# A chunked retention and gated feed-forward kernel: the same operations issued in another order, the gate-value rows in six smaller buffers, seven output buffers

## The chip, the cores and the metric

The kernel runs on one core of a Trainium2 chip. The metric is the device time of one execution in microseconds (us). Before the change three executions took 233.48, 233.62 and 234.39 us, median 233.62 us. Engines are called as in the profile: PE (matrix multiply), PEld (its weight load), DVE, ACT and POOL (elementwise engines), SP (issues transfers only); POOL also issues transfers. Each engine works through its own queue strictly in the order in which it was given its instructions.

## The reference

A retention layer over four sequences of 768 tokens with eight heads of 64, then a normed, gated feed-forward layer without bias over all 3072 tokens:

```python
for t in range(S):                                   # S = 768
    state = gamma * state + einsum('bhd,bhe->bhde', k[:, :, t], v[:, :, t])
    y[:, :, t] = scale * einsum('bhd,bhde->bhe', q[:, :, t], state)
x = y.transpose(0, 2, 1, 3).reshape(B * S, H * D)    # 3072 x 512
xn = x / sqrt(mean(x * x, -1) + 1e-6) * rms_g
g, val = xn @ w_gate, xn @ w_val                     # 512 x 1536 each
out = (g * sigmoid(g) * val) @ w_out                 # 1536 x 512
```

Inputs and output are float32. `gamma` is a constant per head.

## The kernel before

The 768 tokens are cut into six chunks `c` of 128. Per chunk and sequence `b` (0 to 3) the recurrence becomes matrix products. Scores of the chunk (`A`, two PSUM banks per sequence) are masked by DVE (`M0`, `M1`), multiplied with v (`Y`, with the carried state added from chunk 1 on), squared and summed on ACT (`S`), turned into a row factor on POOL (`R`), normed on DVE (`N`) and transposed, by PE and a copy (`X`, `XE`) in chunks 0 and 1, by a transposing transfer of SP (`XE` with `@S`) after that. `K`, `U` and `B` carry the state. Then the feed-forward part of the chunk: gate and value products of 128 hidden columns (`g`, `v`), Silu on ACT (`s`), their product on DVE into the rows `hT` (`h`), the second product (`d`, at the very end `e`), the copy out of PSUM (`o`) and the store (`st`). q and k are loaded (`Lq`, `Lk`), transposed by PE (`Tq`, `Tk`) and copied (`Eq`, `Ek`) in chunks 0 and 1, converted (`Cq`, `Ck`) and transposed by SP's transfers (`tq`, `tk`) later. `D` scales k for the state, `J` transposes one key block back.

Nothing schedules at run time or at build time: a string `ORDER` holds all operations by hand, and a loop at the end of the kernel issues them one after another. `g.0.6.7.0.4/4` is the gate product of chunk 0, hidden blocks 6 to 7, sequences 0 to 4, in PSUM bank 4; `Ck.0.2@D` is a conversion on DVE. The position of an operation in the string is its position in its engine's queue. Waits between engines follow from the data and from the buffers: a ring of n buffers makes the n+1st user wait for the last reader of one of them, and a PSUM bank is free when what lies in it has been read. The operations `H.n` and `hot.n` multiply constants; nobody reads their result, they only keep PE busy where it would be idle.

POOL's queue issues the loads of chunk 0 and 1 and of all weights (`wg`, `wv`, `wo`), which convert to bfloat16 on the way, and does `R`, `B` and some conversions between them. SP's queue issues chunk 2 to 5's loads, the transposing transfers and the stores; the loads of chunk 2 wait until the last part of `wo` has landed (`after`). ACT loads the table of Silu with the operation `tab`.

```python
for w in ORDER.split():
    w, _, bk = w.partition("/")
    w, _, en = w.partition("@")
    f, *a = w.split(".")
    F[f](ENG.get(en), [int(i) for i in bk], *map(int, a))
```

Of the kernel before, what the change touches and what calls it, by code (L numbers as in the profile page):

```python
# [9 lines left out]
F32 = mybir.dt.float32  # L10
BF16 = mybir.dt.bfloat16
AF = mybir.ActivationFunctionType
ALU = mybir.AluOpType
# [4 lines left out]
H.8/3 yt Lk.0.2@S ident Ck.0.2@D vd Lk.1.1@S iota Tk.0.2/0 rms.1@S D.0.2@D Lk.0.0@P Lq.0.1@P H.3/1 Tk.0.0/2  # L18
H.1/1 Tq.0.1/7 Ek.0.0@D mk1 hot.3/1 J.0.0/3 D.0.0@D mk0 Lq.0.0@P Lk.0.1@P Tq.0.0/6 Lq.0.2@P Eq.0.1@A Eq.0.0@A
Tk.0.1/5 Ek.0.1@A Ek.0.2@D yd Lk.0.3@P H.1/1 Tq.0.2/4 tab Lq.0.3@P Eq.0.2@D hot.2/0 A.0.0/5017 M0.0.0 G/2 M1.0.0  # L20
Tq.0.3/6 Lv.0.0@P M0.0.1 GE@A Tk.0.3/3 Eq.0.3@A Lv.0.1@P M1.0.1 Lv.0.2@P Lv.0.3@P wg.0.2 Y.0.0/4 wv.0.2 A.0.2/21
wg.2.4 M1.0.2 Ek.0.3@A Lq.1.1@P H.3/0 A.0.3/61 S.0.0 M0.0.2 H.1/0 Y.0.2/3 K.0.0/0 J.0.1/5 M1.0.3 R.0.0 S.0.2
N.0.0 M0.0.3 Y.0.1/1 H.1/2 X.0.0/4 J.0.3/7 wv.2.4 S.0.1 XE.0.0@D U.0.0@A R.0.2 R.0.1 Ck.1.1@A N.0.2 B.0.0 H.2/2
Y.0.3/0 g.0.0.2.0.1/2 K.0.2/6 S.0.3 s.0.0.2.0.1 N.0.1 U.0.2@A wg.4.6 X.0.2/4 R.0.3 XE.0.2@D D.0.1@D
v.0.0.2.0.1/3 X.0.1/2 wv.4.6 causal XE.0.1@A Lk.1.2@P v.0.0.2.2.3/4 wg.6.9 Lq.1.2@P wv.6.9 h.0.0.2.0.1
g.0.0.2.2.3/6 D.0.3@D Lq.1.0@P g.0.0.2.1.2/5 g.0.2.3.0.3/3 s.0.0.2.2.3 h.0.0.2.2.3 s.0.0.2.1.2 g.0.3.4.0.3/6
N.0.3 v.0.0.2.1.2/4 D.1.1@D Tq.1.1/5 Lk.1.0@P Tk.1.1/0 X.0.3/7 Eq.1.1@D K.0.1/2 wg.9.12 v.0.3.4.0.3/1 Lv.1.1@P
s.0.3.4.0.3 XE.0.3@A g.0.0.4.3.4/6 s.0.2.3.0.3 h.0.0.2.1.2 g.0.4.6.3.4/4 wv.9.12 g.0.4.5.0.3/7 v.0.4.6.3.4/5
v.0.2.3.0.3/3 U.0.1@D s.0.4.6.3.4 Ek.1.1@A h.0.3.4.0.3 g.0.5.6.0.3/0 s.0.4.5.0.3 h.0.4.6.3.4 mc.0@P mc.1@P
# [48 lines left out]
v.3.11.12.0.4/7 h.3.11.12.0.4 K.4.1/4 Lv.5.1@S Y.4.2.2 S.4.1 Y.4.3.2 S.4.2 V.5.1@P d.3.1.0.10/6 tk.5.3 tk.5.2
N.4.0 R.4.1 tk.5.1 st.2.0@S d.3.1.10.12 S.4.3 tq.5.3 N.4.1 R.4.3 o.3.1@A R.4.2 d.3.0.0.10/1 B.4.3 N.4.3 Lq.5.1@S
# [24 lines left out]
def kernel(  # L104
# [530 lines left out]
```

## Time and profile before

| | before |
|---|---|
| time, median of 3 | 233.62 us (233.48 to 234.39) |
| profiled execution, first to last instruction | 233.6 us |
| PE busy | 227.6 us (97%) |
| DVE / ACT / POOL busy | 130.4 / 96.1 / 89.7 us |
| first gate product starts | 19.38 us |
| transfers, mean | 144 GB/s, 33.61 MB |

The profiled execution's span is the median of the timed ones to within 0.1 us, so span and time are used alike. The page shows the busy shares of the engines over time, the clock that PE was granted, and the chain of work that ended last. A busy PE is not a PE at its best: the windows of the profile, which give busy time and clock by stage, and the idle times shown behind an instruction in the order of time say more.

### The profile page before, as it was taken

Reading aid. Unit: us, or ns where it says so; the run is one execution under the profiler, and the core shown is the slowest. Engines: PE = TensorE matmul, PEld = TensorE weight load, DVE = VectorE, ACT = ScalarE, POOL = GpSimd, SP = SyncE. Lnnn points to the kernel's source line nnn. Section 1 sums busy time; section 2 is a strip of 40 time slices with the busy share of each in tenths; the row PEclk is TensorE's granted clock in tenths of the full one; section 3 lists DMA queues with packets and bytes.
Section 4 is the critical chain, followed back from the end, with each engine's and each line's share of the span. In section 5 each row is a group of like instructions: output and inputs, shape, how many; then the busy total and the mean of one; then the engine's idle time right before and its main releaser. Section 6 shows DMA issues by size and latency. Waiting matters only on the chain.

```text
span 233.6 us, 4637 instructions
## 1 busy us (share of the span) xinstructions
PE 227.6 (97%) x1771; PEld 120.8 (52%) x1771; DVE 130.4 (56%) x241; ACT 96.1 (41%) x231; POOL 89.7 (38%) x163
## 2 busy tenths in 40 slices
PE   8799999999999999999999999999999999999994
PEld 2458855645545655445554444554455444444444
DVE  6479639753662965628975239866367532323320
ACT  7658433514337231464731346553265332232202
POOL 8958998550544555030273741247003100000000
PEclk9979999999999999999999999999999999999999
DMA  7999999999798888999988899968511400020222
GB/s 126 147 180 123 127 179 184 205 145 215 133 206 214 171 194 140 262 218 221 235 173 146 179 221 206 198 149 142 148 61 27 112 0 0 3 90 9 83 89 93
DMA packets 105353, 33.61 MB, mean 144 GB/s; under 512 B 94449, under 2 KB 102385, under 8 KB 105330
## 3 DMA queue, kind: packets, MB, share of 16 engines
q1 hardware_dynamic: 81858, 25.70, 50.2%
q0 software_dynamic: 23472, 7.60, 30.1%
q8 instruction: 14, 0.23, 0.4%
q14 instruction: 9, 0.07, 0.1%
HBM read 28.31 MB, written 6.29 MB: 148 GB/s over the span
## 4 chain that ended last, share of the span: by engine, by line
PE 89%; DMA 4%; POOL 2%; ACT 2%; DVE 1%; issue 0%; SPq 0%; POOLq 0%; DVEq 0%; ACTq 0%
PE v_ps L549 27%; PE g_ps L549 27%; PE o_ps L574 21%; PE a_ps L403 3%; DMA kb<-in_k_dram 3%; PE y_ps L441 2%; PE kv_ps L526 2%; PE y_ps L445 2%; DMA out_dram<-o_sb 1%; PE o_ps L596 1%; PE hot_ps L240 1%; PE t_ps L366 1%; PE t_ps L371 1%; PE xt_ps L495 1%; ACT xsq L455 1%; ACT xsq L458 1%
## 5 line engine op out<-in xcount | busy, mean ns | idle before, releaser
L567 DVE TENSOR_TENSOR hT<-sg,v_ps 128x512 bf16<-128x512 bf16 (+2 forms) x76 | 48.7, 656 | 47.8 <-PE v_ps L549 34.8
L549 PE MATMUL v_ps<-xnT,wv_b 128*128 128x512 bf16 (+2 forms) x344 | 71.2, 345 | 0.1
L559 ACT ACTIVATE sg<-g_ps 128x512 bf16<-128x512 f32 (+2 forms) x76 | 42.1, 575 | 70.6 <-PE g_ps L549 68.1
L549 PE MATMUL g_ps<-xnT,wg_b 128*128 128x512 bf16 (+2 forms) x344 | 70.0, 344 | 0.0
L574 PE MATMUL o_ps<-wo_b,hT 128*128 128x512 bf16 x276 | 63.5, 379 | 0.0
L549 PEld LDWEIGHTS <-wg_b 128*128 128x128 bf16 x344 | 30.4, 98 | 29.3
L549 PEld LDWEIGHTS <-wv_b 128*128 128x128 bf16 x344 | 30.2, 98 | 28.9 <-DVE am L426 0.6
L574 PEld LDWEIGHTS <-hT 128*128 128x128 bf16 x276 | 26.3, 98 | 29.1
L468 POOL TENSOR_SCALAR ms<-ssq 128x1 f32<-128x1 f32 x24 | 4.6, 190 | 59.1 <-ACT xsq L458 58.4
L426 DVE TENSOR_TENSOR am<-a_ps,causal 128x512 bf16<-128x512 f32 x32 | 20.6, 685 | 7.8 <-PE a_ps L403 7.5
L339 POOL TENSOR_TENSOR qb<-qf,ydec 128x512 bf16<-128x512 f32 x13 | 14.0, 1074 | 25.2 <-DMA qf<-in_q_dram 24.9
L146 ACT COPY o_sb<-o_ps 128x512 f32<-128x512 f32 (+1 forms) x16 | 8.8, 552 | 29.7 <-PE o_ps L574 23.1
L458 ACT ACTIVATE xsq<-y_ps 128x512 f32<-128x512 f32 x22 | 13.2, 599 | 18.9 <-PE y_ps L445 13.7
L482 DVE SCALAR_TENSOR_TENSOR xn<-y_ps,rstd,g_bc 128x512 bf16<-128x512 f32 x22 | 16.3, 748 | 4.3 <-POOL rstd L470 3.0
L146 DVE COPY o_sb<-o_ps 128x512 f32<-128x512 f32 (+1 forms) x10 | 6.4, 648 | 18.1 <-PE o_ps L574 12.2
L541 POOL CAST st_b<-st_f 64x256 bf16<-64x256 f32 x40 | 15.9, 398 | 1.3
L470 POOL TENSOR_TENSOR rstd<-ms,mhalf 128x1 f32<-128x1 f32 x24 | 13.3, 552 | 2.0
L534 DVE TENSOR_TENSOR st_f<-st_f,kv_ps 128x512 f32<-128x512 f32 x16 | 10.8, 684 | 5.2 <-PE kv_ps L526 4.6
L356 ACT ACTIVATE vp<-vf,vdec 128x64 bf16<-128x64 f32 x48 | 12.2, 343 | 0.0
L426 DVE TENSOR_TENSOR am<-a_ps,mask 128x512 bf16<-128x512 f32 x16 | 10.4, 686 | 2.5 <-PE a_ps L403 2.3
L240 PE MATMUL hot_ps<-one 128*128 128x512 bf16 x20 | 8.5, 547 | 1.1 <-DVE one L153 1.1
L441 PEld LDWEIGHTS <-am 128*128 128x128 bf16 x176 | 7.8, 99 | 3.1 <-issue 0.3
(99 smaller groups left out, 174.8 us busy)
## 6 DMA issues: line engine op xcount, KB each, us to landing
out_dram<-o_sb SPq DMA_DIRECT2D x23, 256.0 KB, 2.4
kf<-in_k_dram SPq DMA_DIRECT2D x18, 256.0 KB, 3.8
qf<-in_q_dram SPq DMA_DIRECT2D x16, 256.0 KB, 3.9
vf<-in_v_dram SPq DMA_DIRECT2D x16, 256.0 KB, 3.9
wo_b<-in_moe_w_out_dram POOLq DMA_DIRECT2D x3, 512.0 KB, 12.2
qb<-in_q_dram POOLq DMA_DIRECT2D x8, 128.0 KB, 6.6
vp<-in_v_dram POOLq DMA_DIRECT2D x8, 128.0 KB, 6.5
kb<-in_k_dram POOLq DMA_DIRECT2D x6, 128.0 KB, 5.9
```

The costliest lines, as they stand in the source:

```text
L146: (e.copy if e is ACT else e.tensor_copy)(out, in_)
L339: e.tensor_tensor(out=u["qb"], in0=u["qf"], in1=ydec[:, c, :, None].to_broadcast([128, H, D]), op=ALU.mult)
L426: DVE.tensor_tensor(out=u["am"][:, i], in0=u["a"][i], in1=m, op=ALU.mult)
L441: nc.tensor.matmul(y[:, h, :], u["am"][:, h % 2, h // 2, :], u["vp"][:, h, :], start=h == 0, stop=c == 0 and h == H - 1, skip_group_check= ...
L458: ACT.activation(xsq, flat(u["y"]), AF.Square, accum_out=u["ssq"])
L470: POOL.tensor_tensor(out=u["rstd"], in0=ms, in1=mhalf, op=ALU.pow)
L482: DVE.scalar_tensor_tensor(out=u["xn"], in0=flat(u["y"]), scalar=u["rstd"], in1=g_bc, op0=ALU.mult, op1=ALU.mult)
L541: POOL.tensor_copy(st_b[b][r, :, i * 64:i * 64 + 64], st_f[b][r, :, i * 64:i * 64 + 64])
L549: nc.tensor.matmul(p[:, (n - n0) * m:(n - n0 + 1) * m], W[w][0][:, s, n * 128:(n + 1) * 128], xnT[c][:, s, b0 * C:b1 * C], start=s == 0, s ...
L559: ACT.activation(sg[:, :cols], done["wg", c, n0, b0][:, :cols], AF.Silu)
L567: DVE.tensor_tensor(out=hT[c][:, n0:n1, b0 * C:b1 * C], in0=sg, in1=p, op=ALU.mult)
L574: nc.tensor.matmul(o_ps[c, b], hT[c][:, n, b * C:(b + 1) * C], wo_b[:, n, :], start=n == 0, stop=n == NFF - 1)
```

## The change

The string `ORDER` is replaced by another one with the same operations, on partly other engines and in other PSUM banks. Three places of the code go with it. The second half of `ident`, a DVE copy that makes `pick` (PE's operand for `Tq` and `Tk` in chunk 0), becomes an operation of its own. The rows `hT` of a chunk, before one tile of 12 blocks in a ring of two, become three tiles of 4 blocks each in a ring of six: the same memory, set free by thirds. The output ring grows from four to seven buffers, and many stores stand much later in SP's queue.

```diff
 ORDER = """
-H.8/3 yt Lk.0.2@S ident Ck.0.2@D vd Lk.1.1@S iota Tk.0.2/0 rms.1@S D.0.2@D Lk.0.0@P Lq.0.1@P H.3/1 Tk.0.0/2
...
+H.1/0 Lk.0.1@P H.1/1 Lk.0.2@S Ck.0.2@A hot.2/2 yt ident H.2/3 Lq.0.0@P vd iota mk1 mk0 H.8/4 Lk.1.1@S rms.1@S Ck.1.1@D
+D.0.2@D pick Tk.0.2/5 G/6 hot.3/7 Ek.0.2@D Lk.0.0@P GE@D Tq.0.0/0 H.1/1 Tk.0.1/2 Tk.0.0/3 Ek.0.1@D Lq.0.1@P Tq.0.1/4
+Lq.0.2@P H.1/5 Lq.0.3@P Lv.0.2@P Tq.0.2/7 Lk.0.3@P Lv.0.0@P Lv.0.3@P Eq.0.0@A Ek.0.0@D J.0.0/6 Lv.0.1@P Eq.0.1@A
...
 """
...
     @op
     def ident_(e, bk):
         make_identity(nc, ident)
+
+    @op
+    def pick_(e, bk):
         DVE.tensor_copy(pick, ident.rearrange("p (s hp i) -> p i hp s", i=2, hp=NHP))
...
+    def h_of(c, r):
+        if (c, r) not in hT:
+            hT[c, r] = ring([128, 4, GT], BF16, "hT", 6)
+        return hT[c, r]
+
     @op
     def h_(e, bk, c, n0, n1, b0, b1):
         m = (b1 - b0) * C
-        if c not in hT:
-            hT[c] = ring([128, NFF, GT], BF16, "hT", 2)
+        r, i = n0 // 4, n0 % 4
         sg, p = (done[w, c, n0, b0][:, :(n1 - n0) * m].rearrange("p (n t) -> p n t", t=m) for w in ("s", "wv"))
-        DVE.tensor_tensor(out=hT[c][:, n0:n1, b0 * C:b1 * C], in0=sg, in1=p, op=ALU.mult)
+        DVE.tensor_tensor(out=h_of(c, r)[:, i:i + n1 - n0, b0 * C:b1 * C], in0=sg, in1=p, op=ALU.mult)
...
     def d(e, bk, c, b, n0, n1):
...
-            nc.tensor.matmul(o_ps[c, b], hT[c][:, n, b * C:(b + 1) * C], wo_b[:, n, :],
+            nc.tensor.matmul(o_ps[c, b], hT[c, n // 4][:, n % 4, b * C:(b + 1) * C], wo_b[:, n, :],
...
     def o(e, bk, c, b, i=None):
...
-            done["o", c, b] = ring([128, DM], F32, "o_sb", 4)
+            done["o", c, b] = ring([128, DM], F32, "o_sb", 7)
...
     def e(e, bk, c, b, i):
...
-            nc.tensor.matmul(p, hT[c][:, n, b * C:(b + 1) * C], wo_b[:, n, CUT[i]:CUT[i + 1]],
+            nc.tensor.matmul(p, hT[c, n // 4][:, n % 4, b * C:(b + 1) * C], wo_b[:, n, CUT[i]:CUT[i + 1]],
```

Three places of the new order bear on the prediction. The first is DVE's queue from the end of the constants to the first copy of the normed rows. `kb` and `kf` are a key block in bfloat16 and as loaded, `kT` and `qT` transposed blocks, `kd` the scaled key block (`D`), `am` masked scores (`M`), `xn` normed rows (`N`), `xnT` their transposed copy (`XE`), `g_bc` the norm's weights. Before:

```order
L250 COPY pick<-ident 128x128
L146 CAST kb<-kf 128x512
L517 TENSOR_TENSOR kd<-kb,vdec 128x512
L146 CAST kT<-t_ps 128x512
L517 TENSOR_TENSOR kd<-t_ps,vdec 128x512
L146 COPY kT<-t_ps 128x512
L146 CAST qT<-t_ps 128x512
L426 TENSOR_TENSOR am<-a_ps,mask_101 128x512 x7
L482 SCALAR_TENSOR_TENSOR xn<-y_ps,rstd,g_bc 128x512
L426 TENSOR_TENSOR am<-a_ps,mask_101 128x512
L146 COPY xnT<-xt_ps 128x4x128
L482 SCALAR_TENSOR_TENSOR xn<-y_ps,rstd,g_bc 128x512 x2
```

In the new order the same stretch of DVE's queue reads:

```order
L142 CAST kb<-kf 128x512
L516 TENSOR_TENSOR kd<-kb,vdec 128x512
L249 COPY pick<-ident 128x128
L142 COPY kT<-t_ps 128x512
L142 COPY g_bc<-g_row_ps 128x512
L142 CAST kT<-t_ps 128x512 x2
L516 TENSOR_TENSOR kd<-t_ps,vdec 128x512
L425 TENSOR_TENSOR am<-a_ps,mask_101 128x512 x7
L481 SCALAR_TENSOR_TENSOR xn<-y_ps,rstd,g_bc 128x512
L425 TENSOR_TENSOR am<-a_ps,mask_101 128x512
L481 SCALAR_TENSOR_TENSOR xn<-y_ps,rstd,g_bc 128x512 x2
L142 COPY xnT<-xt_ps 128x4x128
```

`pick` stands behind a scaled key block, the norm's weights and a second key copy came to DVE from ACT, a query copy left, and the first copy of normed rows stands behind three norms where it stood behind one.

The second place is the start of POOL's queue (`pos_i`, `row_i`, `ident` and `row_m` are constants). Before:

```order
L168 IOTA row_i 128x128
masks.py:197 MEMSET ident 128x128
masks.py:199 AFFINE_SELECT ident<-ident 128x128
L244 AFFINE_SELECT row_m<-row_f 128x128
L312 DMA kb<-in_k_dram 128x1x512
L312 DMA qb<-in_q_dram 128x1x512 x2
L312 DMA kb<-in_k_dram 128x1x512
```

And now:

```order
L164 IOTA row_i 128x128
L311 DMA kb<-in_k_dram 128x1x512
masks.py:197 MEMSET ident 128x128
masks.py:199 AFFINE_SELECT ident<-ident 128x128
L311 DMA qb<-in_q_dram 128x1x512
L240 AFFINE_SELECT row_m<-row_f 128x128
L311 DMA kb<-in_k_dram 128x1x512
L311 DMA qb<-in_q_dram 128x1x512 x3
```

The first load went ahead of `ident` and `row_m`, which now stand between it and the third. The first four loads are the four blocks of the first two sequences in both orders, in another succession (`Lk.0.1`, `Lq.0.0`, `Lk.0.0`, `Lq.0.1` now), and `Lq.0.2` is the fifth in both.

The third place is POOL's queue where the weights' loads meet the first row factors (`ms` and `rstd`, the two instructions of `R`). Before:

```order
L323 DMA wv_b<-in_moe_w_val_dram 128x4x256
L323 DMA wg_b<-in_moe_w_gate_dram 128x4x256
L314 DMA qb<-in_q_dram 128x8x64
L468 TENSOR_SCALAR ms<-ssq 128x1
L470 TENSOR_TENSOR rstd<-ms,mhalf 128x1
L323 DMA wv_b<-in_moe_w_val_dram 128x4x256
```

And now:

```order
L322 DMA wv_b<-in_moe_w_val_dram 128x4x256
L322 DMA wg_b<-in_moe_w_gate_dram 128x4x256
L322 DMA wv_b<-in_moe_w_val_dram 128x4x256
L467 TENSOR_SCALAR ms<-ssq 128x1
L469 TENSOR_TENSOR rstd<-ms,mhalf 128x1
L467 TENSOR_SCALAR ms<-ssq 128x1
```

A fourth weight load stands ahead of the first row factor in place of a query load; three row factors then follow one another ahead of the next load, and the fourth stands behind that one.

More of the change, by code (lines that the diff above doesn't have):

```diff
@@ new lines @@
+Lq.1.0@P s.0.6.7.0.4 Ek.1.2@A wv.9.12 Tq.1.1/7 wo.0.4 causal Lv.1.2@P Lq.1.3@P wo.4.8 B.0.3 B.0.1 s.0.8.9.0.4
+h.0.8.9.0.4 v.0.6.7.0.4/0 Eq.1.1@D v.0.7.8.0.4/1 Lv.1.3@P wo.8.12 Lv.2.2@S s.0.7.8.0.4 Lk.2.2@S h.0.7.8.0.4
+h.0.6.7.0.4 g.0.10.11.0.4/2 A.1.2/65 Tq.1.0/3 Lq.2.1@S B.0.2 Lv.2.0@S Eq.1.0@D s.0.10.11.0.4 g.0.11.12.0.4/4
+s.0.11.12.0.4 Lq.2.2@S g.0.9.10.0.4/7 Lv.1.1@P mc.0@P A.1.0/1203 v.0.9.10.0.4/4 M0.1.2 mc.1@P M1.1.2 Lq.2.0@S Lv.1.0@P
+v.0.10.11.0.4/6 v.0.11.12.0.4/5 s.0.9.10.0.4 Lk.2.1@S M0.1.0 M0.1.1 d.0.0.0.4/7 M1.1.1 M1.1.0 h.0.11.12.0.4
@@ new lines @@
+s.1.0.4.3.4 tq.2.1 h.1.0.4.3.4 g.1.4.5.0.4/7 V.2.3@D v.1.7.8.0.4/3 B.1.3 Ck.2.0@A s.1.4.5.0.4 g.1.7.8.0.4/0 tk.2.0
+s.1.7.8.0.4 Lk.2.3@S h.1.7.8.0.4 Ck.2.1@D g.1.9.10.0.4/4 s.1.9.10.0.4 h.1.9.10.0.4 B.1.0 v.1.0.1.0.3/6 Cq.2.2@D
+V.2.2@D U.1.1@D g.1.1.2.0.3/5 Lk.3.0@S tq.2.0 s.1.1.2.0.3 v.1.4.5.0.4/7 Ck.2.2@A g.1.3.4.0.3/0 s.1.3.4.0.3
+g.1.0.1.0.3/3 g.1.8.9.0.4/4 g.1.2.3.0.3/2 h.1.4.5.0.4 g.1.6.7.0.4/5 tk.2.1 v.1.3.4.0.3/1 Ck.2.3@D s.1.0.1.0.3
+v.1.1.2.0.3/0 h.1.0.1.0.3 K.2.3/7 h.1.3.4.0.3 Ck.3.0@A h.1.1.2.0.3 K.2.2/3 Lq.3.0@S U.2.2@D U.2.3@D tq.2.2
@@ new lines @@
+v.2.1.2.0.4/0 Lv.3.3@S Ck.3.2@P h.2.1.2.0.4 Y.3.0/6 Lk.5.2@S S.3.0 v.2.4.5.0.4/1 g.2.8.9.0.4/5 N.3.1 o.1.2@A
+g.2.3.4.0.4/3 Ck.4.1@A R.3.0 tq.4.0 N.3.0 tq.3.2 s.2.8.9.0.4 v.2.8.9.0.4/0 g.2.6.7.0.4/4 Lk.4.0@S V.3.3@A B.3.0
+g.2.7.8.0.4/7 tk.3.3 h.2.8.9.0.4 v.2.7.8.0.4/6 Lk.4.2@S Lq.4.2@S v.2.3.4.0.4/5 h.2.4.5.0.4 s.2.3.4.0.4 v.2.2.3.0.4/0
+tk.3.2 st.1.2@S s.2.7.8.0.4 h.2.7.8.0.4 v.2.6.7.0.4/1 h.2.3.4.0.4 B.3.1 Lv.4.0@S B.2.3 K.3.3/3 U.3.3@D Ck.4.2@A
+s.2.6.7.0.4 Ck.4.0@A h.2.6.7.0.4 g.2.9.10.0.4/7 g.2.5.6.0.4/6 Cq.4.2@P s.2.2.3.0.4 h.2.2.3.0.4 v.2.5.6.0.4/4
@@ new lines @@
+st.1.0@S XE.5.2@S o.3.3@D R.5.1 st.3.1@S st.3.3@S g.4.1.2.0.4/4 v.4.6.7.0.4/2 h.4.6.7.0.4 g.4.4.5.0.4/5 h.4.10.11.0.4
+N.5.1 g.4.3.4.0.4/0 v.4.4.5.0.4/6 v.4.3.4.0.4/2 s.4.5.6.0.4 v.4.11.12.0.4/7 XE.5.3@S s.4.1.2.0.4 h.4.11.12.0.4
+s.4.4.5.0.4 h.4.4.5.0.4 g.4.2.3.0.4/3 s.4.3.4.0.4 st.3.0@S v.4.5.6.0.4/4 g.4.0.1.0.4/1 g.4.7.8.0.4/7 h.4.5.6.0.4
+h.4.3.4.0.4 s.4.0.1.0.4 v.4.9.10.0.4/5 v.4.2.3.0.4/6 g.4.9.10.0.4/4 v.4.1.2.0.4/0 s.4.2.3.0.4 h.4.1.2.0.4
+g.4.8.9.0.4/1 XE.5.0@S XE.5.1@S v.5.4.5.0.4/2 h.4.2.3.0.4 s.4.9.10.0.4 s.4.7.8.0.4 v.4.7.8.0.4/3 h.4.7.8.0.4
@@ new lines @@
+v.5.8.9.0.4/2 h.5.7.8.0.4 s.5.0.1.0.4 h.5.0.1.0.4 h.5.3.4.0.4 v.5.11.12.0.4/1 d.4.3.0.12/0 g.5.11.12.0.4/6 s.5.8.9.0.4
+g.5.10.11.0.4/4 d.4.0.10.12 h.5.8.9.0.4 s.5.10.11.0.4 v.5.10.11.0.4/3 d.5.0.0.10/5 d.5.1.0.10/2 s.5.11.12.0.4
+h.5.11.12.0.4 h.5.10.11.0.4 d.5.0.10.12 d.5.2.0.12/4 st.4.1@S o.5.2@A o.5.0@D st.5.0@S st.3.2@S d.5.1.10.12
+d.4.2.0.12/6 o.4.0@D e.5.3.1/1 o.5.1@D st.4.0@S st.5.2@S st.5.1@S o.4.3@D st.4.3@S o.4.2@D st.4.2@S e.5.3.2/3
+o.5.3.2@A st.5.3.2@S o.5.3.1@A st.5.3.1@S e.5.3.0/5 o.5.3.0@D st.5.3.0@S
```

131 lines of the change are left out of this document (50 added, 81 removed).

## The prediction

> **What bounds the kernel now.** I read the page first, for its busy shares.
>
> ```profile
> span 233.6 us, 4637 instructions
> ...
> PE 227.6 (97%) x1771; PEld 120.8 (52%) x1771; DVE 130.4 (56%) x241; ACT 96.1 (41%) x231; POOL 89.7 (38%) x163
> ...
> PEclk9979999999999999999999999999999999999999
> ```
>
> PE is busy for 97% and no other engine for more than 56%. A new order that gives PE the same work can win at most the 6 us in which PE is idle, and whatever constant work (`H`, `hot`) and low clock cost it. So the second view is the busy time by stage. Its columns are the stretch, its length, then the busy time of PE, PEld, DVE, ACT and POOL, the granted clock, the share of the transfer engines, and GB/s.
>
> ```profile
> 5.97:9.39 3.42, 2.33 (x58) 1.48 (x56) 1.68 (x3) 2.39 (x7) 3.42 (x5) 1.00 1.03 142
> 9.39:12.80 3.41, 3.05 (x56) 1.74 (x58) 1.91 (x4) 2.31 (x4) 3.18 (x5) 1.00 1.86 154
> 12.80:16.20 3.40, 3.40 (x54) 1.94 (x53) 2.58 (x5) 2.22 (x5) 1.27 (x4) 0.50 1.85 182
> 16.20:19.38 3.18, 3.13 (x54) 2.20 (x54) 2.75 (x5) 2.14 (x6) 1.76 (x5) 1.00 1.69 186
> 19.38:60.00 40.62, 40.62 (x401) 25.81 (x398) 26.46 (x47) 16.87 (x38) 27.18 (x43) 1.00 1.34 165
> 60.00:120.00 60.00, 60.00 (x465) 31.89 (x464) 38.44 (x63) 27.98 (x72) 23.87 (x44) 1.00 0.94 204
> 120.00:180.00 60.00, 59.76 (x429) 29.70 (x428) 36.13 (x59) 24.72 (x68) 23.11 (x45) 1.00 0.71 146
> 180.00:230.50 50.50, 50.46 (x264) 24.29 (x260) 16.49 (x26) 12.85 (x25) 0.74 (x2) 1.00 0.17 53
> ```
>
> From 19.38 us, where the first gate product starts, to 230.50 PE is idle for 0 + 0 + 0.24 + 0.04 = 0.28 us, at the full clock. Nothing can be won there; it can only be lost. All that can be won lies ahead of 19.38, where the third stretch ran at half clock. So the third view is the chain of work that ended last, over the start (start, length, what).
>
> ```profile
> 1.00 0.24 POOL row_i L168
> ...
> 2.08 0.76 POOL kb L312
> ...
> 3.85 5.85 DMA kb<-in_k_dram
> ...
> 9.75 0.44 PE t_ps L366 x16
> ...
> 10.52 0.37 PE t_ps L366 x16
> ...
> 13.79 0.54 PE y_ps L441 x8
> ...
> 14.87 1.39 PE hot_ps L240 x3
> ...
> 17.18 0.70 ACT xsq L458 x2
> ```
>
> The start is set by POOL's loads of q, k and v (the fourth, issued up to 3.85, lands at 9.70), and then by one trip through all engines: scores, mask, first product `Y`, squares `S`, row factor `R`, norm `N`, transpose `X`.
>
> **The frame of the sum.** PE's matrix products are the same 1771 before and after, so what counts is which of them stand ahead of the first gate product. The order puts `K.0.2`, `Tk.1.1`, `X.0.1` and `X.0.2` ahead of it that stood behind, and `J.0.1` behind it that stood ahead; each is four products of 128 columns. In the order of time on PE the distances between starts price them:
>
> ```profile
> 19.38 0.61 PE L549 MATMUL g_ps<-xnT,wg_b 128*128 128x128 bf16 x8
> 19.82 0.39 PE L526 MATMUL kv_ps<-vp,kd 128*128 128x128 bf16 x4
> 20.05 0.39 PE L495 MATMUL xt_ps<-ident,xn 128*128 128x128 bf16 x4
> 20.27 0.61 PE L549 MATMUL v_ps<-xnT,wv_b 128*128 128x128 bf16 x8
> ```
>
> `K` takes 20.05 - 19.82 = 0.23, a transpose 0.22, eight products of the feed-forward 0.44. Net three such groups move forward, 0.67 us. If the first gate product starts at T, and nothing waits behind it that did not wait before, the new time is 233.6 + (T - 20.05). The break-even is 19.38 + 0.67 = 20.05.
>
> **The loads.** POOL's first load goes ahead of `ident` and `row_m`. It can be issued at the end of `row_i`, 1.00 + 0.24 = 1.24 in place of 2.08. The two constants now stand between it and the third load, so if the issue sets the pace, the fourth and later ones gain nothing; if each transfer waits for those ahead of it, all gain 0.84 us.
>
> ```profile
> vp<-in_v_dram POOLq DMA_DIRECT2D x8, 128.0 KB, 6.5
> ```
>
> The v loads, issued last, take longer to land (6.5 us) than the fourth load (5.85 us): the transfers do queue up, so some of the 0.84 is carried on. `A.0.0` (scores) stands behind the transpose of the fifth load, `Tq.0.2`, in both orders (row 10.52). That is 9.68 at the earliest, and with 0.37 for it and four transposes of `J.0.0` (0.22) `A.0.0` starts between 10.3 and, as before, 11.1. I take 10.7.
>
> The Trainium skill (DMA: Bandwidth & Descriptors, "Anatomy of one DMA — SWDGE (gpsimd) path") puts such a load at about 2.0 us plus its bytes by 436 GB/s; a float32 source of 256 KB would take an estimated 2.6 us, less than half of the 5.85 us in the row. By it the loads would not limit and T would come some 2 us earlier; the trace of before speaks against it, and its outcome lies with the first rival below.
>
> **From the scores to the first gate product.** These rows give the links:
>
> ```profile
> 8.40 0.69 DVE L517 TENSOR_TENSOR kd<-t_ps,vdec 128x512 bf16<-128x512 bf16 x1 [0.49 <-PE t_ps L510]
> 11.61 2.48 DVE L426 TENSOR_TENSOR am<-a_ps,mask 128x512 bf16<-128x512 f32 x4
> 17.24 0.74 DVE L482 SCALAR_TENSOR_TENSOR xn<-y_ps,rstd,g_bc 128x512 bf16<-128x512 f32 x1
> 18.50 0.42 DVE L146 COPY xnT<-xt_ps 128x512 bf16<-128x512 bf16 x1
> ...
> 11.06 1.28 ACT L287 ACT_TABLE_LOAD   x1
> 18.52 0.58 ACT L146 COPY st_f<-kv_ps 128x512 f32<-128x512 f32 x1
> ...
> 15.16 0.19 POOL L468 TENSOR_SCALAR ms<-ssq 128x1 f32<-128x1 f32 x1 [2.04 <-ACT xsq L458]
> 15.43 0.58 POOL L470 TENSOR_TENSOR rstd<-ms,mhalf 128x1 f32<-128x1 f32 x1
> ```
>
> `Y.0.0` started at 13.79. It needs v of sequence 0, now the ninth load in place of the eighth, and two masks of 2.48 / 4 = 0.62 behind `D.0.0` of 0.69: I put it at 12.95 (0.84 earlier) to 13.79. New is that `K.0.2` and the two copies `U.0.0` and `U.0.2` stand ahead of `S.0.0`. The first copy runs beside `Y`; the second comes after `Y` and `K.0.2`, at 0.54 + 0.23 after the start of `Y` (the half clock's price for `Y`). Then 0.58 for the copy, 0.70 for `S` (row 17.18), 15.43 + 0.58 - 15.16 = 0.85 for `R`: `N.0.0` starts 2.90 after `Y`, at 15.85 to 16.69. DVE is then just done with its seven masks (0.69 + 7 x 0.62 = 5.03 from about 10.7 on, so 15.7), so they cost nothing; if `R` came earlier they would hold it. Then `N.0.0` 0.74 and `M0.0.3` 0.62 on DVE: 17.2 to 18.05.
>
> Two paths lead on. PE has `Y.0.3`, `X.0.0`, three constant products, `X.0.1`, three more, `X.0.2` and `J.0.3`: five groups of 0.22 and two of 0.65 (as four products of 384 columns, the same 1536, in the row 28.83 below), 2.4 us, to 19.6 to 20.45. DVE has two more norms and the copy, 2 x 0.74 + 0.42 = 1.9, to 19.1 to 19.95. PE's is the longer, and `N.0.1` and `N.0.2` end ahead of their transposes. T is 19.6 to 20.45, and the sum has left out the handing on between engines at some eight places: between the two instructions of `R` it shows as 15.43 - 15.16 - 0.19 = 0.08. I take T = 20.2, in the upper half. This term is 20.2 - 20.05 = +0.15, bounds -0.75 (T = 19.3, if `Y` starts earlier still) and +0.8.
>
> **Silu's table.** The load of 1.28 us at 11.06 lay beside other work. Now it stands right ahead of the first Silu, behind the copy `XE.0.1`. ACT has until PE needs that PSUM bank again, at `K.0.1`, which stands two gate or value products of 0.22 x 2 and some four of 0.65 later, 3.3 us behind T. Table load plus Silu (0.58 at most) end 1.4 us ahead of that. I cost it at nothing; if that cover were gone it would be worth up to 1.28.
>
> **The weights.** POOL issues them between its row factors.
>
> ```profile
> 15.97 0.83 POOL L323 DMA_DIRECT2D wv_b<-in_moe_w_val_dram  x1
> 20.46 0.81 POOL L323 DMA_DIRECT2D wg_b<-in_moe_w_gate_dram  x1
> 24.11 0.76 POOL L323 DMA_DIRECT2D wg_b<-in_moe_w_gate_dram  x1
> ...
> 28.83 0.65 PE g_ps L549 x4
> ...
> 31.24 1.80 PE g_ps L549 x8
> ...
> PE t_ps L366 <- DMA kb<-in_k_dram: 1.4, 2, 1.0
> ...
> SPq L314 <- DMA wo_b<-in_moe_w_out_dram: 48.0, 1, 48.0
> ```
>
> The load issued at 24.11 feeds the gate products of block 6, which began at 31.24 (chain). PE waited nowhere for a weight: of the transfers it waited for a key alone (`t_ps <- kb`). In the new order those gate products stand 9.2 us behind T, so at 29.4: eight groups of 0.44, six of 0.65, four of 0.22, one of 0.89. Their load stands behind `R.0.3` and one key load. With `R.0.3` near 19.9 it is issued at 20.7 to 21.5, and if it takes what it took, at most 31.24 - 24.11 = 7.1 us, it lands at 27.8 to 28.6. That is 0.8 to 1.6 ahead. The other pieces of weights, reckoned in the same way, are a microsecond or two ahead as well. The bounds for all waits behind T are 0 and 1.5 us (one weight late by as much as it is now early); I take 0.25, nearer to the row in which PE waited for none. SP's queue is held for `wo`, 48.0 us, in both orders.
>
> **Buffers and the end.** `hT` set free by thirds and seven output buffers can only shorten waits, and behind 19.38 PE has 0.28 us of them: 0 to -0.28, taken 0. The later stores in SP's queue pass transposing transfers, whose results PE does not wait for by the stretches above: 0, with the bound of 1.5 already given. The last copy of the output goes from ACT to DVE:
>
> ```profile
> 230.50 0.32 ACT L146 COPY o_sb<-o_ps 128x192 f32<-128x192 f32 x1 [1.29 <-PE o_ps L596]
> ```
>
> A copy of 0.32 us and the store, 233.6 - 230.50 = 3.1 us in all, follow PE's end either way: 0, within 0.1. The sum is 233.6 + 0.15 + 0.25 = 234.0 us. The span equals the median of the three runs, so it stands for the time too.
>
> **Rivals.** The first ends faster: the loads come earlier by more than the 0.84, because a transfer that starts in a shorter queue also lands sooner. Then `Y` waits for its masks alone: `D.0.0` from 10.3 on, 0.69 + 2 x 0.62, so 12.25; and in a start without gaps the clock stays full through 16.2, so `Y` takes 0.23 and not 0.54. T = 12.25 + 2.59 + 0.74 + 0.62 + 2.4 = 18.6, and the time 233.6 - 1.45 = 232.2. For it speaks that landing slows down along the queue, 5.85 to 6.5 us; against it that 182 GB/s flow from 12.80 on and only 142 ahead of 9.39, so these loads are not held by the amount of data. It decides if v of sequence 0 lands before 12.3.
>
> The second ends slower through the clock. In the stretches above it went to 0.50 at 12.80, after a stretch with 3.05 us of PE work, most of it transposes of 64 columns and waits, and came back at 16.20 after 3.40 us of unbroken work. The rows allow the reading that it is set anew every 3.4 us by how full the array was. The new order has fewer constant products between 9.4 and 18, and if the half clock also holds from 16.2 to 19.6, the 2.4 us of PE's path cost up to 1.3 more in that stretch: 235.3. If it holds up to 23.0, 3.4 / 2 = 1.7 more: 237.0. Against it: the masks and norms, not PE, set much of that path. It decides if the clock is still 0.50 at 17.
>
> The Trainium skill (TensorE: Matmul & The Clock Gate, "What's actually happening") says that free-running windows of 3.41 us decide between half and full clock by how busy PE was. The switches in the rows, 3.4 us apart and to 0.50, agree.
>
> The third ends slower through the weights: POOL issues nothing while it waits for ACT's squares, and four `R` ahead of the load for block 6 put it at 22.5 in place of 21; `S` on ACT stands behind two copies and the table. It lands at 29.6 to 30.5 and PE waits 0.3 to 1.2 there, and as much again for the next pieces behind it in the queue: 235 to 236. It decides if that load is issued later than 22.2.
>
> **How the numbers follow.** My own case, ending within 0.5% of before (232.45 to 234.79; less than this cannot be told from no change), gets 0.44: two opposite shifts of under a microsecond, and covers that hold. The faster rival 0.20, the clock 0.16, the weights 0.20. The likeliest is 234.0; its own range is 232.9 (T = 19.3, no later wait) to 235.2. The range for all is 232.0 to 236.2: it leaves out about 0.06 of the faster rival beyond 232.0 and some 0.1 where the clock stays low up to 23.0 or two late terms add. So faster 0.20, same 0.44, slower 0.36.
>
> **What would show it.** Right: the first POOL load issued near 1.2; `A.0.0` at 10.3 to 11.1; `Y.0.0` at 12.95 to 13.8; the first gate product at 19.6 to 20.5; from there to PE's end under 0.6 us of idle time and the clock at 1.00; Silu's table load between the first gate products with no wait of PE behind it; the gate products of block 6 starting within 9.2 to 9.6 us of the first. Wrong: a gate product before 19.0; half clock past 16.2; PE waiting for `wg_b` or `wv_b`, or anywhere between 60 and 180 us for a transposing transfer, where I have read the order but no row shows the new margins.

## The result and the profile after

The changed kernel takes 237.69 us (median of four runs, 237.46 to 237.88) against 233.8 us of the kernel before beside it: a ratio of 1.0162, with a 95% interval of 1.0136 to 1.0189. It is 3.9 us slower, and the time lies above the predicted range of 232.0 to 236.2. The page of its profiled execution, whose own time was 237.88 us:

```profile
span 236.1 us, 4620 instructions
...
PE 227.0 (96%) x1771; PEld 121.1 (51%) x1771; DVE 136.9 (58%) x247; ACT 92.1 (39%) x215; POOL 86.1 (36%) x159
...
PEclk9997999999999999999999999999999999999999
```

The spans differ by only 2.5 us (236.1 and 233.6) where the times differ by 3.9. The dip of the clock stands in the fourth slice now, and in the third before. The windows of the changed kernel, with the columns of those before (PE, PEld, DVE, ACT, POOL, granted clock, transfers):

```profile
14.00:16.00 2.00, 1.49 (x29) 0.98 (x28) 1.96 (x4) 2.00 (x6) 0.56 (x2) 1.00 1.48 195
16.00:18.00 2.00, 0.35 (x9) 0.36 (x10) 1.76 (x3) 0.91 (x4) 1.54 (x5) 0.96 1.45 196
18.00:20.00 2.00, 2.00 (x14) 1.18 (x12) 1.40 (x4) 0.69 (x2) 1.82 (x5) 0.50 0.84 104
20.00:21.74 1.74, 1.74 (x14) 0.96 (x12) 0.64 (x2) 1.44 (x3) 1.74 (x3) 0.64 1.10 142
21.74:60.00 38.26, 38.26 (x372) 23.99 (x370) 25.46 (x44) 13.35 (x31) 25.01 (x40) 1.00 1.49 193
60.00:120.00 60.00, 59.69 (x462) 31.95 (x459) 43.07 (x69) 26.98 (x59) 22.17 (x42) 1.00 0.90 172
120.00:180.00 60.00, 59.29 (x439) 29.90 (x438) 34.87 (x56) 25.10 (x71) 21.58 (x43) 1.00 0.70 158
180.00:232.90 52.90, 52.89 (x269) 25.30 (x267) 17.85 (x27) 12.25 (x23) 0.00 (x0) 1.00 0.15 53
```

PE is busy for 0.35 of the 2 us from 16 to 18, then works at half clock up to 21.25, just ahead of the first gate product at 21.74. Behind it PE is idle for 0.31 + 0.71 + 0.01 = 1.03 us, where the kernel before had 0.28. In the order of time on PE around the dip:

```profile
17.64 0.48 PE L440 MATMUL y_ps<-vp,am 128*128 128x64 bf16 x8 [1.82 <-DVE am L425]
...
18.35 1.49 PE L236 MATMUL hot_ps<-one 128*128 128x512 bf16 x3
...
20.05 1.40 PE L236 MATMUL hot_ps<-one 128*128 128x512 bf16 x3
...
21.74 0.44 PE L548 MATMUL g_ps<-xnT,wg_b 128*128 128x128 bf16 x5
```

PE stands still for 1.82 us in front of `Y.0.3`, for the mask `M0.0.3`. The two groups `H.3` then last 1.28 and 1.24 us (18.35 to 19.63, where `X.0.1` starts, and 20.05 to 21.29, where `X.0.2` starts), twice the 0.65 of the full clock. Among the waits of PE that the profile of before does not have are these:

```profile
PE y_ps L440 <- DVE am L425: 1.8, 1, 1.8
...
PE y_ps L435 <- DVE hT L570: 0.5, 1, 0.5
...
PE v_ps L548 <- DVE xnT L142: 0.3, 1, 0.3
...
PE y_ps L435 <- ACT xsq L454: 0.2, 1, 0.2
```

Between the two profiles the sum closes: the first gate product is 21.74 - 20.05 = 1.69 later than its break-even, PE idles 0.75 us more behind it, together 2.44 of the 2.5. What is left open by them is the other 1.4 us, by which the times differ more than the spans.

### The profile page after: what moved, and what is told of

Its sections match the earlier page's. It is cut to its first block, busy times and chain, and to the rows that moved or that the text cites. A ratio compares the mean times of both kernels' runs of the same rounds, so it can differ in the third digit from the quotient of the medians.

```text
span 236.1 us, 4620 instructions
## 1 busy us (share of the span) xinstructions
PE 227.0 (96%) x1771; PEld 121.1 (51%) x1771; DVE 136.9 (58%) x247; ACT 92.1 (39%) x215; POOL 86.1 (36%) x159
## 4 chain that ended last, share of the span: by engine, by line
PE 88%; POOL 3%; DMA 3%; ACT 2%; DVE 2%; issue 1%; POOLq 0%; ACTq 0%
PE v_ps L548 26%; PE g_ps L548 26%; PE o_ps L577 24%; DMA vp<-in_v_dram 3%; PE a_ps L402 2%; PE y_ps L440 2%; PE kv_ps L525 2%; PE y_ps L444 2%; PE o_ps L599 1%; PE hot_ps L236 1%; ACT xsq L457 1%; POOL qb L311 1%; PE t_ps L370 1%; POOL rstd L469 1%; PE xt_ps L494 1%
## 5 line engine op out<-in xcount | busy, mean ns | idle before, releaser
L570 DVE TENSOR_TENSOR hT<-sg,v_ps 128x512 bf16<-128x512 bf16 (+2 forms) x76 | 48.2, 656 | 49.2 <-PE v_ps L548 30.7
L548 PE MATMUL v_ps<-xnT,wv_b 128*128 128x512 bf16 (+2 forms) x344 | 70.2, 344 | 0.3 <-DVE xnT L142 0.3
L540 POOL CAST st_b<-st_f 64x256 bf16<-64x256 f32 x40 | 16.7, 416 | 20.9 <-DVE st_f L533 9.0
L481 DVE SCALAR_TENSOR_TENSOR xn<-y_ps,rstd,g_bc 128x512 bf16<-128x512 f32 x22 | 16.4, 748 | 10.5 <-POOL rstd L469 10.3
L142 ACT COPY o_sb<-o_ps 128x512 f32<-128x512 f32 (+2 forms) x15 | 7.9, 547 | 31.4 <-PE o_ps L577 23.4
L338 POOL TENSOR_TENSOR qb<-qf,ydec 128x512 bf16<-128x512 f32 x11 | 11.4, 1043 | 21.8 <-DMA qf<-in_q_dram 17.1
L142 DVE COPY o_sb<-o_ps 128x512 f32<-128x512 f32 (+1 forms) x11 | 7.1, 657 | 11.6 <-PE o_ps L577 8.4
L440 PE MATMUL y_ps<-vp,am 128*128 128x64 bf16 x176 | 8.8, 194 | 2.2 <-DVE am L425 1.8
L236 PE MATMUL hot_ps<-one 128*128 128x512 bf16 x20 | 8.0, 536 | 1.1 <-DVE one L149 1.1
```

The costliest lines, as they stand in the source:

```text
L142: (e.copy if e is ACT else e.tensor_copy)(out, in_)
L338: e.tensor_tensor(out=u["qb"], in0=u["qf"], in1=ydec[:, c, :, None].to_broadcast([128, H, D]), op=ALU.mult)
L440: nc.tensor.matmul(y[:, h, :], u["am"][:, h % 2, h // 2, :], u["vp"][:, h, :], start=h == 0, stop=c == 0 and h == H - 1, skip_group_check= ...
L481: DVE.scalar_tensor_tensor(out=u["xn"], in0=flat(u["y"]), scalar=u["rstd"], in1=g_bc, op0=ALU.mult, op1=ALU.mult)
L540: POOL.tensor_copy(st_b[b][r, :, i * 64:i * 64 + 64], st_f[b][r, :, i * 64:i * 64 + 64])
L548: nc.tensor.matmul(p[:, (n - n0) * m:(n - n0 + 1) * m], W[w][0][:, s, n * 128:(n + 1) * 128], xnT[c][:, s, b0 * C:b1 * C], start=s == 0, s ...
```

## The experiments

All ratios are to the kernel before, run beside each experiment. Its medians lie between 233.70 and 234.17 there, so between experiments the ratios compare better than the times. The diffs of `ORDER` show parts of lines.

**The kernel before, for its spans.** Nothing is edited.

> The kernel before, unchanged, timed beside itself. It is here for its spans: the profile shows a span 2.5 us shorter than that of the changed kernel, the times differ by 3.9 us. If the span of 233.6 us was an unlucky execution of before, its other spans lie near 231.8 us, and its time is its span plus about 1.9 us, as in the changed kernel; if the span is typical, about 233.6 us again, and the changed kernel loses 1.4 us outside of its span. Ratio 1.000.

Over all the runs of the study, 103 executions of the kernel before have a span and a time. The time is the span plus 1.94 us (median, 1.66 to 2.12), and the median span is 232.0 us, with a clock of 1.00. In nine of the 103 the mean clock is 0.993, as in the profile shown of before; these take 235.24 us (median) where the 89 at 0.998 and more take 233.75. (Five more, at 0.984 to 0.991, take 236.3 to 237.9.) The profile taken in this run is of that kind as well: its span is 233.1, the clock is at half from 11.8 to 15.2, and the first gate product starts at 18.56. For the profile shown of before, 233.6 us with 3.4 us at half clock, 1.94 around the span gives an estimated time of 235.5, not 233.6. The changed kernel's time is also its span plus 1.8 to 2.1, so nothing is lost outside its span, and all four of its runs have a clock of 0.992 or 0.993. What is rare in the kernel before is the rule in the changed one.

**The order of before with the new buffers.** The old `ORDER` in the new code (the operation `pick` behind `ident`).

> The order of before with the buffers of the change: six buffers of a third for hT, seven for the output. Theory: nothing waits for these buffers behind 19.38 us, so it stands at 1.000 of before, within 0.2%. Rival, the buffers themselves cost something (other addresses, other waits): slower by 0.5% or more, which would be a third of what the change lost.

The ratio to before is 0.9975, interval 0.9943 to 1.0008: the buffers cost nothing, as forecast, and win nothing that can be told. Its profile is also one of the usual executions of the old order:

```profile
9.39:12.80 3.41, 3.41 (x80) 2.10 (x76) 2.96 (x6) 3.18 (x7) 3.41 (x5) 1.00 2.26 160
12.80:16.20 3.40, 3.40 (x56) 2.10 (x53) 3.35 (x6) 2.40 (x7) 1.93 (x5) 1.00 1.56 188
16.20:19.38 3.18, 3.12 (x54) 2.72 (x52) 3.00 (x6) 3.09 (x9) 2.85 (x7) 1.00 1.63 174
```

The clock is 1.00 where the profile of before had 0.50, and the first gate product starts two us ahead of the 19.38 against which the forecast reckoned:

```profile
17.37 0.44 PE L552 MATMUL g_ps<-xnT,wg_b 128*128 128x128 bf16 x5
```

The half clock is not all of these two us. In the profile of before the scores `A.0.0` were already late ahead of the dip, at 11.04 where they start at 10.28 here, since PE had waited 1.01 us for a key load. In the half-clock profile of the experiment above they start at 10.22 and the first gate product at 18.56. So about 1.2 of the two us are the dip and 0.8 the load.

**The gap in front of `Y.0.3` filled.**

```diff
-S.0.1 R.0.1 M1.0.3 Y.0.2/1 N.0.0 S.0.2 R.0.2
+S.0.1 R.0.1 M1.0.3 Y.0.2/1 H.6/0 N.0.0 S.0.2 R.0.2
```

> Six constant products of 512 columns are added in front of Y.0.3, where PE waits 1.8 us for a mask (16 to 17.6 us). Clock theory: the idle time there is what sends the clock to half from 17.9 to 21.3 us; with PE filled it stays at 1.00, the two H.3 take 0.65 in place of 1.26 each and the transposes 0.22 in place of 0.43, so the first gate product starts near 20.3 in place of 21.74 and the kernel is 1.3 to 1.6 us faster than the changed one. Rival, that the norms set the start: it stays within 0.3 us of 21.74, or PE loses 1.3 us more.

236.29 us, a ratio of 1.0100 (1.0071 to 1.0129) where the changed kernel had 1.0162: more work on PE makes it 1.4 us faster. The windows (14.4 to 21.2) and PE's order of time:

```profile
14.40:17.80 3.40, 2.85 (x36) 1.65 (x37) 2.88 (x6) 2.16 (x8) 2.55 (x7) 1.00 1.44 195
17.80:21.20 3.40, 3.40 (x50) 2.83 (x48) 2.81 (x6) 2.98 (x8) 3.24 (x6) 1.00 1.02 126
```

```profile
15.14 1.45 PE L236 MATMUL hot_ps<-one 128*128 128x512 bf16 x6 [0.15 <-ACT kT L142]
17.00 0.41 PE L440 MATMUL y_ps<-vp,am 128*128 128x64 bf16 x8 [0.40 <-DVE am L425]
...
17.47 0.81 PE L236 MATMUL hot_ps<-one 128*128 128x512 bf16 x3
18.12 0.39 PE L494 MATMUL xt_ps<-ident,xn 128*128 128x128 bf16 x4
...
19.43 0.33 PE L548 MATMUL g_ps<-xnT,wg_b 128*128 128x128 bf16 x3
```

The clock stays at 1.00, `H.3` takes 18.12 - 17.47 = 0.65, and the clock is 0.997 to 1.000 in all seven executions. From `Y.0.3` to the first gate product it is 19.43 - 17.00 = 2.43 us, where the changed kernel took 4.10. That the idle time sends the clock down is shown; it is worth 1.4 us in the times and 1.67 in this stretch of the traces. The Trainium skill (TensorE: Matmul & The Clock Gate, "What's actually happening") has an idle window of about 3.4 us lead to half clock. The trace of the changed kernel agrees on the length, with 3.41 us at half clock from 17.84 to 21.25, but not on the idle window: PE worked for 1.26 us in the 3.41 us ahead of it.

**Both `H.3` left out.** The six products that nobody reads, ahead of `X.0.1` and `X.0.2`, are gone.

> Both H.3 ahead of the first gate product are left out (6 products that nobody reads). If the clock is decided by the idle time before 17.8 alone, it is half again from 17.9 to 21.3, the first gate product starts at about 19.9 in place of 21.74 and the gate products up to 21.3 run at half speed, 0.7 us lost: 1.2 us faster than the changed kernel in all. If the clock needs these products to come back at 21.3, it stays at half up to 24.7: another 1.7 us lost, 0.5 us slower than the changed kernel. If the clock plays no part, 1.3 us faster with no half clock at the gate products.

237.11 us, ratio 1.0113 (1.0058 to 1.0168, four executions): 0.6 us faster than the changed kernel by the medians and 1.1 by the ratios, too uncertain to tell 0 from 1.2. The windows say more:

```profile
14.40:17.80 3.40, 1.32 (x26) 0.91 (x24) 3.40 (x7) 2.45 (x8) 2.06 (x6) 0.92 1.45 196
17.80:21.20 3.40, 3.40 (x41) 3.27 (x39) 2.58 (x6) 2.86 (x6) 3.08 (x6) 0.58 0.84 109
21.20:24.60 3.40, 3.40 (x50) 2.88 (x48) 2.55 (x5) 2.20 (x7) 3.40 (x5) 1.00 1.22 106
```

The half clock lies at 17.3 to 20.7 in this profile; it comes back without the constant products, after a stretch in which PE was busy nearly throughout. The first gate product starts at 19.67 and its 8 products take 0.85 in place of 0.44: what the missing products win, the half clock takes back in part.

**The two later places.** `Y.4.3.2` ahead of `S.4.2` again, and `XE.1.1` ahead of three other instructions on DVE; then the first of the two alone; then the same pair turned round in the kernel before.

```diff
-B.4.0 M1.4.3 M0.4.3 Y.4.2.2 S.4.2 Y.4.3.2 tq.5.1
+B.4.0 M1.4.3 M0.4.3 Y.4.2.2 Y.4.3.2 S.4.2 tq.5.1
...
-XE.1.0@A o.0.2@D Cq.2.1@D U.1.0@D XE.1.1@D
+XE.1.0@A XE.1.1@D o.0.2@D Cq.2.1@D U.1.0@D
```

> The changed kernel with two of its later places undone: Y.4.3.2 again stands ahead of S.4.2 (both sequences share two PSUM banks, so PE waits for ACT's squares of the one before it writes the other), and the copy XE.1.1 stands ahead of an output copy, a query conversion and a state update on DVE. Theory: these two places are all that the changed kernel loses behind its first gate product, 0.7 + 0.5 us in its trace: 1.0 to 1.2 us faster than the changed kernel (237.7), so 236.5 to 236.7, PE idle for under 0.3 us behind the first gate product. Rival, the waits move on to the next instruction: 237.3 or more. The start is untouched: half clock in 17.9 to 21.3.

> The changed kernel with one edit: Y.4.3.2 ahead of S.4.2. In the trace of the changed kernel PE stands still 0.7 us at this pair (155.1 to 155.5 us). Theory: PE waits there for ACT's squares because both sequences lie in the same two banks; 0.7 us faster than the changed kernel (237.0), and 120 to 180 us without idle time. Rival, the wait is for DVE and stays: 237.7.

> The kernel before with the same edit the other way round: S.4.2 put ahead of Y.4.3.2. Theory: PE waits 0.5 to 0.7 us for ACT where it did not, 0.2 to 0.3% slower than before. Rival, that it matters in the changed kernel's neighbourhood alone: the same as before within 0.1%.

With both: 235.78 us, ratio 1.0086 (1.0051 to 1.0120). With the pair alone: 236.59 us, ratio 1.0101 (1.0071 to 1.0132). The trace with both has no idle time behind the first gate product:

```profile
21.20:60.00 38.80, 38.80 (x383) 24.53 (x381) 25.62 (x45) 14.11 (x32) 26.57 (x42) 1.00 1.49 194
60.00:120.00 60.00, 60.00 (x450) 31.62 (x448) 42.71 (x69) 27.00 (x60) 22.21 (x43) 1.00 0.87 178
120.00:180.00 60.00, 60.00 (x444) 30.22 (x443) 34.14 (x55) 24.88 (x69) 20.74 (x41) 1.00 0.67 154
```

The times say 1.9 and 1.1 us, the idle time in the trace of the changed kernel 1.03 and 0.71. The edits do not touch the start, yet the start differs too: the first gate product is at 20.72 and 20.87 in these two profiles, 1.02 and 0.87 earlier than in that of the changed kernel, and half of the ten executions with both had the full clock there. So the larger numbers are not the price of the waits alone. In the kernel before, the pair turned round gives 234.2 us, ratio 1.0024 (1.0000 to 1.0047; no change is at its edge), with this wait in its list:

```profile
PE y_ps L436 <- ACT xsq L455: 0.8, 2, 0.6
```

and 60 - 59.23 = 0.77 us of idle PE time from 120 to 180, where the profile of before had 0.24. The row of the changed kernel names DVE's `hT` for most of this wait; the runs show that it was ACT's `S.4.2`.

**The start put back, step by step.** From the version with the filled gap: `X.0.0` ahead of `Y.0.3`, its copy ahead of the next norms, the first gate and value products ahead of `X.0.1`, no `H.3`.

```diff
-N.0.0 S.0.2 R.0.2 wg.2.4 M0.0.3 Y.0.3/5 S.0.3 N.0.1 R.0.3 X.0.0/4 Lk.1.3@P H.3/0 X.0.1/6
-N.0.2 wg.6.9 H.3/3 X.0.2/2 J.0.3/7 XE.0.0@D g.0.0.2.0.1/1 J.0.1/0 v.0.0.2.0.1/4 N.0.3 XE.0.2@D XE.0.1@A
+N.0.0 S.0.2 R.0.2 wg.2.4 M0.0.3 X.0.0/4 Y.0.3/5 S.0.3 XE.0.0@D N.0.1 R.0.3 Lk.1.3@P
+g.0.0.2.0.1/0 v.0.0.2.0.1/4 X.0.1/6 N.0.2 wg.6.9 X.0.2/2 J.0.3/7 J.0.1/1 XE.0.2@D N.0.3 XE.0.1@A
```

> The kernel with six constant products ahead of Y.0.3, and its start after that put back in the manner of before: X.0.0 ahead of Y.0.3, its copy ahead of the next norms, the first gate and value products ahead of X.0.1 and X.0.2, both H.3 left out. Theory: of what remains there (236.3), 1.3 to 1.5 us are PE's constant products and transposes ahead of the first gate product; it then starts near 17.5 in place of 19.4, with three groups less ahead of it (0.67), and a few tenths of idle time between X.0.1 and X.0.2: 235.0 to 235.4. Rival, that weights or norms are late anyway: PE idles behind the first gate product for what it won, 236.0 or more. Clock 1.00 throughout.

235.36 us, ratio 1.0057 (1.0028 to 1.0086), 0.9 us less; the first gate product starts at 17.85. With the two later places undone as well:

> Both of the above: the filled gap with the start put back, and the two later places undone. If the three terms (clock 1.4, products ahead of the first gate product 1.2, later waits 1.1) are separate and are all there is, they add up: 237.7 - 3.7 = 234.0, within 0.4 of the kernel before. If they hide one another, 234.8 or more.

234.81 us, ratio 1.0039 (1.0014 to 1.0064). The terms do not add up to the whole; 1.06 us stay. Then `S.0.0` ahead of the two state copies:

```diff
-K.0.0/0 U.0.0@A Y.0.0/3 K.0.2/1 U.0.2@A S.0.0
+K.0.0/0 Y.0.0/3 K.0.2/1 S.0.0 U.0.0@A U.0.2@A
```

> As the last, and the squares S.0.0 stand ahead of the two state copies U.0.0 and U.0.2 on ACT. The forecast charged 0.58 us and more for these copies on the chain to the first norm. In the trace DVE waits 0.3 to 0.5 us for the first row factor, so S.0.0 earlier by 1.07 brings N.0.0 forward by those 0.3 to 0.5 us only (then the masks end last): 0.3 to 0.5 us faster than the run without it. If the masks or v's landing set it: within 0.1.

234.30 us, ratio 1.0006 (0.9974 to 1.0038): 0.5 us less by the medians, as expected, though the two intervals overlap. By the ratio the version stands level with the kernel before; the medians, 234.30 and 233.75, are still 0.55 apart. In its trace DVE no longer waits for the first row factor, for which it waited 0.20 us without the edit:

```profile
15.66 0.74 DVE L481 SCALAR_TENSOR_TENSOR xn<-y_ps,rstd,g_bc 128x512 bf16<-128x512 f32 x1
```

**Silu's table earlier**, in that version: `yd tab` behind `S.0.2` in place of ahead of `s.0.0.2.0.1`.

> The version with the start put back, the two later places undone and S.0.0 ahead of the copies, and in addition Silu's table loaded earlier, behind S.0.2, where ACT is idle for 1.2 us. The forecast costed the table at nothing because of the cover of 1.4 us. PE waits there 0.2 us for a Silu and 0.3 for a copy of the norm. Theory: 0.2 us faster than without (234.3), so 234.1. Rival, S.0.3 comes later behind the table and what was won is lost at X.0.3: 234.3 to 234.6.

234.37 us, ratio 1.0025 (1.0004 to 1.0047) against 1.0006: no gain. Of the two waits that were to go, the 0.2 us for a Silu is gone from its trace and the 0.3 us for a copy of the norm is still there (0.26 us, against 0.27 without the edit). Another stands there, which is not in the trace without the edit:

```profile
PE kv_ps L525 <- POOL vp L357: 0.9, 1, 0.9
```

It stands at 131 to 133 us, far from the edit, in this and in two other profiles of edited new orders (0.6 to 0.9 us), and not in that of the changed kernel: a late conversion on POOL that some executions have. What sets it was not tried.

**The first load alone.** The kernel before with `Lk.0.0` ahead of `ident` on POOL.

> The kernel before with its first load on POOL ahead of ident and row_m, as in the changed kernel, and nothing else. The forecast left open whether the later loads gain the 0.84 us (each waits for those ahead of it) or nothing (the issue sets the pace). Theory after the traces: nothing, since A.0.0 starts at 10.1 to 11.2 with the early load and at 10.2 to 11.0 without: 1.000 of before, within 0.1%. Rival: the queue runs ahead by 0.4 to 0.84 us and the kernel is 0.2 to 0.35% faster.

234.61 us, ratio 1.0023 (0.9993 to 1.0053): nothing won. On POOL the first load is issued at 1.44 in place of 2.08, 0.64 us earlier and not 0.84. The two constants then follow it, so the second is issued at 3.03 (2.83), the fourth at 4.05 (3.85) and the fifth at 4.65 in both. In PE's order of time of this kernel:

```profile
9.14 0.44 PE L366 MATMUL t_ps<-pick,kb 128*64 128x64 bf16 x16 [0.61 <-DMA kb<-in_k_dram]
...
9.83 0.44 PE L366 MATMUL t_ps<-pick,qb 128*64 128x64 bf16 x16
```

`Tq.0.2`, on the fifth load, starts at 9.83; in the four profiles of the old order with the late first load it starts at 9.63, 9.64, 9.69 and 10.45. The transpose on the first load, at 6.20, lies among theirs as well (5.99 to 7.03), and so does the wait for the fourth load, 0.61 us here and up to 1.01 there. The landings differ more between executions than by the edit.

## Why the prediction was wrong

**The frame was wrong by 1.9 us, and it was the largest error.** "The span equals the median of the three runs, so it stands for the time too" is the sentence that failed. A time is its span plus 1.94 us here, and the profile of before shows a rare execution with a half clock: its span of 233.6 stands beside a usual one of 232.0. That it equalled the median of the times was chance. The forecast of 234.0 is a span, to be compared with 233.6; as a time it would have been about 235.9. The profile had shown 3.4 us at half clock just ahead of the first gate product, and the forecast took them as the kernel's property. With the full clock and no late key load the old order starts its first gate product at 17.37, so the break-even was 18.04 and not 20.05.

**The term of the start: the mechanism up to `Y.0.3` right, the size behind it wrong.** Scores, first product and norm came inside their bounds (`A.0.0` 10.97 of 10.3 to 11.1, `Y.0.0` 13.40 of 12.95 to 13.79, `N.0.0` 16.24 of 15.85 to 16.69), and `Y.0.3` started at 17.64, where masks and norm were put at 17.2 to 18.05. Part of this is luck: in the profiles of the edited versions, whose orders are the same up to there, `A.0.0` starts anywhere from 10.10 to 11.22. The step that failed is "five groups of 0.22 and two of 0.65, 2.4 us": it took 21.74 - 17.64 = 4.1 us, 3.4 of it at half clock. At the full clock, with the gap filled, it took 2.43, so the groups were priced rightly and the clock was not. The forecast's own sum had PE waiting for DVE up to 17.2 at the least, with no work to fill it, and did not ask what that gap does to the clock; only its second rival came near to it.

**The clock rival was the one that happened**, though not at the time it named: the clock was not low at 17, it was full until 17.84 and fell because of the gap. Its price of 1.3 was near the 1.4 that filling the gap won; its chance of 0.16 was too low.

**Of the loads, the bound of 0 was the true one.** In the kernel before, the early first load won nothing at the fifth, which was issued no earlier. In the changed kernel too the first is issued at 1.44, not 1.24, and the fourth at 4.01, against 3.85 before. By the price of the Trainium skill (DMA: Bandwidth & Descriptors, "Anatomy of one DMA — SWDGE (gpsimd) path") the forecast had the start some two us earlier; no run shows that.

**The state copies** on the way to the first norm were charged rightly: from `Y.0.0` to `N.0.0` it took 16.24 - 13.40 = 2.84 us, put at 2.90. Taking them off it gave 0.5 us by the medians.

**The waits behind the first gate product** were put at 0.25 with bounds 0 and 1.5; the idle time was 1.03, 0.75 more than before. The places were not the ones that were looked at. Weights were in time, as forecast: block 6 was issued at 20.75 and its gate products began 31.00 - 21.74 = 9.26 us behind the first. No transposing transfer was waited for. What was missed is `S.4.2` between two products that share their PSUM banks, 0.7 us, and a copy behind three other instructions on DVE, 0.3 us of wait. Both can be read in the order.

**Buffers, table and end were rightly costed at nothing:** the buffers 0.9975 with 1 inside the interval, no PE wait at the table, 3.2 us behind PE's last product against 3.1.

So of the 3.9 us, taken out one after another, the half clock accounts for 1.4, the constant products and transposes ahead of the first gate product for 0.9, the later waits for 0.6 (their idle time in the changed kernel is 1.03) and the state copies for 0.5, together 237.69 - 234.30 = 3.4. The ratio is then back at 1.0006 (0.9974 to 1.0038); whether the 0.5 us left between the medians is a loss stays open. No version is faster than the kernel before by more than its interval.

## What to carry to other kernels

Before reckoning against one profile, see whether it is a usual execution: compare its span plus the overhead with the timed runs, and do not take a dip of the clock in it as given. A wait of PE of under two us can cost more than itself, here another 1.4 us at half clock behind it; filling it with products that nobody reads is cheap, while the same products on the path ahead of the first real work are not. When work is reordered, look for instructions of other engines that now stand between two users of the same PSUM bank.

## What was unexpected of the hardware

PE's busy time alone did not decide the clock. In the profile of before, where the dip from 12.80 to 16.20 marks off stretches of 3.4 us, 2.33 us of PE work from 5.97 to 9.39 was followed by the full clock, and 3.05 us from 9.39 to 12.80 by the half. In the changed kernel 1.26 of 3.41 us was followed by the half. With the gap filled 2.85 of 3.40 kept it full (14.4 to 17.8), as did 2.55 in the version with the start put back and the later waits undone; where the clock's own stretches lie in a run without a dip is not known.

The transposes of 64 columns, to which the second rival pointed, do not tell the two stretches of before apart: they are 48 of the 58 products in the one that kept the clock, and 35 of the 56 in the one that lost it. The longest item of the latter is the product that spreads the norm's weights, whose operands have a single row (`1*128`):

```profile
11.69 1.12 PE L296 MATMUL g_row_ps<-g_row,ones 1*128 1x512 f32 x2
```

It starts within the 3.4 us ahead of the dip in the other two half-clock profiles of the old order as well. It is also in the full-clock ones, where its place in the clock's stretches is not known. Whether it counts for less than other work was not tried.
